# Windowed attention into an ELU feed-forward: one input load behind another gate, two value copies a step later, one subtraction behind two copies

## The chip, the cores and the metric

The kernel runs on one core of one Trainium2 chip. The metric is the device time of one execution in microseconds (us); three runs of the kernel before are given with their median. A profiled execution has its own time and, within it, a span from the first instruction to the last.

## The reference

The inputs are q, k and v of shape 8 x 8 x 576 x 64 (batch, heads, positions, width) in float32, and two matrices w_in (512 x 2048) and w_out (2048 x 512). Cut to what matters:

```
scores = q @ k.T / sqrt(64);  only |i - j| <= 32 is kept
attn = exp(scores) / sum(exp(scores));  y = attn @ v
x = y of all heads side by side: 4608 tokens x 512
h = x @ w_in
g = h where h > 0, else exp(min(h, 0)) - 1
out = g @ w_out            # 4608 x 512, float32
```

## The kernel before, in words

**Attention.** A batch has nine blocks of 64 query rows. Two blocks make a pair `i`, so 36 pairs cover the 8 batches, and four and a half pairs are one batch. `scores(i)` multiplies a 128-key window with the 64 queries of each block on TensorE (PE), for eight heads. `exponential(i)` is one exp on ScalarE (ACT), `mask(i)` multiplies with the band mask on VectorE (DVE), `pv(i)` multiplies with the values on PE, and `normalize(i)` divides by the sums on DVE. The result `x_st` is transposed, by PE for the first pairs (`x_transpose`, and a copy `x_evac` out of PSUM), later by DMA.

Even and odd blocks need the values at row offsets that differ by 64. So the values exist twice in SBUF: `V_e`, loaded by GpSimd's DMA queue with a conversion to bf16 (`load_v`, five parts for a batch), and `V_o`, the same rows moved by 64 partitions. `rotate_v(b, m0, m1, parts)` makes `V_o` with DVE copies (line 176); its part z of the copy reads parts m0 + z to m1 + z of `V_e`. `hold_v` is a tiny DVE write into `V_e` that a following `load_v` has to wait for, which sets the time at which GpSimd issues that load.

Queries and keys come in float32 through SyncE's DMA queue (`load_qk`, two transfers for each call, one for even and one for odd heads), are cast to bf16 (`cast_qk`) and transposed (`transpose_qk`) on PE for the early batches. Batch 1 comes in two parts: `ONE_A` through GpSimd's queue with a conversion, and `ONE_B`, the second part, in float32 through SyncE's queue.

**Feed-forward.** Tokens go in 18 tiles of 256. A tile has 8 steps, each of which takes 256 of the 2048 hidden columns. There are 144 steps `kk`; `order` lists which tile and which columns a step has. The first 16 steps mix tiles 0 and 1, ending with (tile 0, columns 7) at step 14 and (tile 1, columns 7) at step 15. In a step `mm1` (products, line 755) makes h in a PSUM bank; ACT makes exp(h) (`exponents`, line 764); DVE (ACT in three early steps) subtracts one (`subtract`, line 775) and `elu` (line 786) takes min and max into bf16 `g_sb`. Two steps later `mm2` adds g @ w_out into the tile's sums `psY` (line 806); after a tile's last `mm2`, `rows_out` copies both halves of the sums out of PSUM, one on ACT and one on DVE, and SyncE's queue writes them to memory. The h banks are `h0` and `h1`, by the parity of the step. Pair scores use bank pairs `s` and `u`; the bank pair `u` is lent to tile 1's sums (`h2` and `t0`) from step 5 to step 18 (`swap_pools`, `swap_back`).

**Order of the work.** Nothing is scheduled automatically: each engine runs its instructions in the order in which the program issues them. The loop over `kk` runs, in this order: the tasks "first", `elu` of the step before, the tasks "dve", `mm1` of this step with the tasks "half" in its middle, the tasks "mid", `mm2` of the step two before, and the tasks "end". `at(kk, slot, fn, ...)` puts a task into such a slot. So step 14's "mid" holds the cast of batch 1's second queries (on ACT), step 15's "mid" that of its keys (on DVE), and the ends of steps 15 and 16 hold their transposes; pairs 6 and 7 are scored in the middle of step 18.

**Gates.** The loads of the weights (`load_w_in`, `load_w_out`, in halves of quarters) and of batch 1's values are issued by GpSimd in a fixed order. `gate(src)` is a DMA of one element on SyncE's queue that reads `src`; as SyncE's queue waits for the landing of what the gate reads, everything behind it on this queue is issued only after that. In the kernel before one gate on the last column of w_in's fourth quarter (`w_in_at(3)`) stands ahead of the loads of batch 1's second part and of batch 2:

```python
    gate(w_in_at(3))
    for which in range(2):
        load_qk(1, which, ONE_B)
    for which in range(2):
        load_qk(2, which, WHOLE)
```

Of the kernel before, what the change touches and what calls it, by code (L numbers as in the profile page):

```python
# [15 lines left out]
def _bap(ap, new_ap, off=0):  # L16
    return bass.AP(tensor=ap.tensor, offset=ap.offset + off,
                   ap=[list(x) for x in new_ap])
# [3 lines left out]
def kernel(  # L22
# [15 lines left out]
    D_MODEL = H * D  # L38
# [8 lines left out]
    VS = 5  # L47
# [5 lines left out]
    NFO = D_FF // 128  # L53
# [56 lines left out]
    w_out_sb = wpool.tile([128, NFO, D_MODEL], BF16, name="w_out_sb")  # L110
# [10 lines left out]
    ONE_A, ONE_B = (0, HJ - 1), (NC * (HJ - 1), HJ + 1)  # L121
    qk_f = {}

    def load_qk(b, which, part, engs=(nc.sync, nc.sync)):
        z, nj = part
        mj = max(nj, HJ + 1)
        t = lpool.tile([128, 2, mj * D], FP32, tag=f"f{which}{mj}",
                       name=f"f{which}", bufs=2 if part is WHOLE else 1)
        qk_f[b, which, z] = t
        src = (q, k)[which][b, :, z:z + NC * nj, :].rearrange(  # L130
            "(g h) (c j) d -> c g h (j d)", h=2, j=nj)
        for h in range(2):
            engs[h].dma_start(out=t[:, h, 0:nj * D], in_=src[:, :, h, :])
# [14 lines left out]
    def load_v(b, m, rows=(0, 128)):  # L148
        lo = 128 * m - WIN
        p0 = max(rows[0], -lo)  # L150
        p1 = min(rows[1], S - lo)
        nc.gpsimd.dma_start(  # L152
            out=V_e[b % 3][p0:p1, m, :, 0:D],
            in_=v[b, :, lo + p0:lo + p1, :].rearrange("h p d -> p h d"))
# [37 lines left out]
    def gate(src, dt=BF16, eng=nc.sync):  # L192
        gates[0] += 1
        t = cpool.tile([1, 1], dt, name=f"gate{gates[0]}")
        eng.dma_start(out=t, in_=src)
# [17 lines left out]
    def w_in_at(c):  # L213
        return w_in_sb[0:1, 0, (c + 1) * (D_FF // 4) - 1:(c + 1) * (D_FF // 4)]
# [7 lines left out]
    def edges(i, eng=nc.vector):  # L222
        eng.memset(V_e[i][:, :, :, D:VD], 1.0)
        eng.memset(V_e[i][0:32, 0], 0.0)
        eng.memset(V_e[i][96:128, VS - 1], 0.0)
        if i < 2:
            for c0, n in ((KPAD - WIN, HP), (KPAD + HP * S, 1)):
                z = kT[i][:, c0:c0 + WIN]
                nc.vector.memset(_bap(z, [z.ap[0], [S, n], [1, WIN]]), 0.0)
# [328 lines left out]
        load_v(1, 2 + z)  # L558
    load_v(1, 4)
    edges(2, nc.gpsimd)  # L560
    gate(w_in_at(3))
    for which in range(2):
        load_qk(1, which, ONE_B)
    for which in range(2):
        load_qk(2, which, WHOLE)

# [5 lines left out]
    def at(kk, slot, fn, *args):  # L572
        tasks.setdefault((kk, slot), []).append((fn, args))
# [24 lines left out]
    def transpose_casts():  # L598
        elu(8)
        n, (nq, nk) = ONE_A[1], (c[1] for c in FRONT_C)  # L600
        pt = ps_tile([128, 2048], BF16, "s", "ptx")
        evicts = []
        for b, which, part, lo in ((0, 0, FRONT_C[0], n),
                                   (0, 1, FRONT_C[1], n + nq),
                                   (1, 0, ONE_A, 0)):
            transpose_qk(b, which, part, 0, part[1], nc.vector, later=evicts,
                         pt=pt[:, lo * 128:(lo + part[1]) * 128])
        pk = ps_tile([128, 1024], BF16, "h0", "ptx")
        transpose_qk(1, 1, ONE_A, 0, n, nc.scalar, later=evicts, pt=pk)
        for evict in evicts:  # L610
            evict()
# [11 lines left out]
        at(16 + m, "mid", load_v, 2, m)  # L623
    at(12, "dve", rotate_v, 1, 0, 1)
    for z in range(2):
        at(14 + z, "dve", rotate_v, 1, 1, VS - 1, (z,))

# [4 lines left out]
    for i in range(4, NPAIR):  # L634
        two = i >= FIRST_TWO
        kk, z = begin[i], i % 2 if two else 0
# [69 lines left out]
    def mm1(kk):  # L706
        t, s = order[kk]
        if kk == BY_PAIRS[1]:
            return
        ks = BY_PAIRS if kk == BY_PAIRS[0] else (kk,)  # L710
        tags = ((f"h{kk % 2}", "s") if kk == NSTEP - 1 else
                ("s",) if kk == 2 else ("u",) if kk == 3 else (f"h{kk % 2}",))
        for k in ks:
            psH[k] = []
        rows = 128 if kk >= BY_ROWS else TT
        for z, tag in enumerate(tags):
            for k in ks:
                psH[k].append(ps_tile([128, FG * TT // rows // len(tags),
                                       rows], FP32,
                                      tag if k == kk else "u", "ps"))  # L720
        for p in range(len(ks)):
            for k in ks:
                for z in range(len(tags)):
                    products(k, z, p if len(ks) > 1 else None)
                if p == len(ks) - 1:
                    for z in range(len(tags)):
                        exponents(k, z)
                        if k == NSTEP - 1:
                            elu(k, z)
# [31 lines left out]
    def exponents(kk, z):  # L761
        ps = psH[kk][z]
        e_sb = mpool.tile(list(ps.shape), FP32, tag="e_sb", name="e_sb")
        nc.scalar.activation(e_sb, ps, AX.Exp)  # L764
        e_t[kk, z] = e_sb
        if kk > 0:
            subtract(kk, z)

    def subtract(kk, z):
        e_sb = e_t.pop((kk, z))  # L770
        m_sb = mpool.tile(list(e_sb.shape), BF16, tag="m_sb", name="m_sb")
        if kk in (1, 3, 4):
            nc.scalar.activation(m_sb, e_sb, AX.Copy, bias=-1.0)
        else:
            nc.vector.tensor_scalar(m_sb, e_sb, -1.0, None, ALU.add)  # L775
        m_t[kk, z] = m_sb

    def elu(kk, z=0):
        ps = psH[kk][z]
        w, rows = ps.shape[1:]  # L780
        if z == 0:
            g_t[kk] = mpool.tile([128, FG * TT // rows, rows], BF16,
                                 tag="g_sb", name="g_sb", bufs=8)
        if kk == 0:
            subtract(kk, z)
        nc.vector.scalar_tensor_tensor(  # L786
            g_t[kk][:, z * w:(z + 1) * w, :], ps, 0.0, m_t.pop((kk, z)),
            ALU.max, ALU.min)
# [69 lines left out]
    for kk in range(NSTEP):  # L858
        run(kk, "first")
        for n in {1: (), 2: (0, 1), 9: ()}.get(kk, (kk - 1,)):  # L860
            if n >= 0:
                elu(n)
        run(kk, "dve")
        mm1(kk)
        run(kk, "mid")
        if kk == NSTEP - 1:
            last_sums()
        elif kk >= LATE + LAG:
            for _ in range(3 if kk < LATE + LAG + 4 else 4):
                add(*todo.pop(0))  # L870
        else:
            for n in {2: (), 3: (), 4: (), 5: (0, 2), 6: (1, 3), 7: (4,),
                      8: (5, 6)}.get(kk, (kk - LAG,) if kk >= LAG else ()):
                run(kk, n)
                mm2(n)
        run(kk, "end")
# [30 lines left out]
```

## Time and profile before

| | |
|---|---|
| median of three runs | 301.27 us (301.15 to 303.06) |
| the profiled execution's own time | 304.11 us |
| its span | 302.4 us |
| PE busy | 290.8 us, 96% |
| DVE busy | 240.7 us, 80% |
| ACT busy | 169.0 us, 56% |
| GpSimd busy | 56.5 us, 19% |
| granted clock of TensorE | full |

A busy share is an average over stages with different limits. The chain that ended last (PE 81%, DMA 11% of it) and the waits of single instructions tell what a stage is bound by. In the profile L755 and L806 are the products and the sums, L764 the exponent, L775 the subtraction, L786 the minimum and maximum, L291 and L293 copies and casts on ACT and on DVE, L341 and L385 PE's transposes and scores, L133 the float32 loads, L152 the value loads, L195 a gate. q0 is the queue of the DMAs that GpSimd issues, q1 that of SyncE and ACT. PEld is the loading of weights into TensorE, which overlaps the matmuls.

### The profile page before, as it was taken

Reading aid. Unit: us, or ns where it says so; the run is one execution under the profiler, and the core shown is the slowest. Engines: PE = TensorE matmul, PEld = TensorE weight load, DVE = VectorE, ACT = ScalarE, POOL = GpSimd, SP = SyncE. Lnnn points to the kernel's source line nnn. Section 1 sums busy time; section 2 is a strip of 40 time slices with the busy share of each in tenths; the row PEclk is TensorE's granted clock in tenths of the full one; section 3 lists DMA queues with packets and bytes.
Section 4 is the critical chain, followed back from the end, with each engine's and each line's share of the span. In section 5 each row is a group of like instructions: output and inputs, shape, how many; then the busy total and the mean of one; then the engine's idle time right before and its main releaser. Section 6 shows DMA issues by size and latency. Waiting matters only on the chain.

```text
span 302.4 us, 7697 instructions
## 1 busy us (share of the span) xinstructions
PE 290.8 (96%) x3080; PEld 198.2 (66%) x3132; DVE 240.7 (80%) x478; ACT 169.0 (56%) x256; POOL 56.5 (19%) x81
## 2 busy tenths in 40 slices
PE   7799998999999999999999999999999999999996
PEld 3476666677666666666666666666666666666764
DVE  7676787878888887988798879887888777777773
ACT  3774447778664567546753675377635363634342
POOL 8778611820004100230013001400000000000000
PEclk9999999999999999999999999999999999999999
DMA  9999999999965997999799969996941121121011
GB/s 192 170 190 164 186 222 410 374 165 201 200 196 148 297 121 198 261 310 149 134 259 287 237 154 274 315 171 118 259 81 72 35 72 36 72 37 69 2 69 70
DMA packets 94790, 52.74 MB, mean 174 GB/s; under 512 B 78243, under 2 KB 84643, under 8 KB 94755
## 3 DMA queue, kind: packets, MB, share of 16 engines
q0 software_dynamic: 45552, 10.03, 44.8%
q1 hardware_dynamic: 47330, 35.68, 44.7%
q10 hardware_dynamic: 1872, 6.55, 6.2%
q8 instruction: 24, 0.39, 0.5%
q14 instruction: 12, 0.09, 0.1%
HBM read 36.70 MB, written 15.34 MB: 172 GB/s over the span
## 4 chain that ended last, share of the span: by engine, by line
PE 81%; DMA 11%; POOL 3%; issue 2%; DVE 1%; ACT 1%; SPq 0%; POOLq 0%; DVEq 0%; ACTq 0%
PE ps L755 38%; PE psY L806 36%; DMA w_in_sb<-in_moe_w_in_dram 6%; PE psS L417 3%; PE psS L385 3%; DMA c<-in_q_dram 2%; DMA f<-in_q_dram 2%; POOL Vo L159 1%; PE ptx L341 1%; PE psXT L439 0%; POOL c L146 0%; DVE y_sb L293 0%; ACT e_sb L764 0%; DVE g_sb L786 0%; DVE m_sb L775 0%
## 5 line engine op out<-in xcount | busy, mean ns | idle before, releaser
L755 PE MATMUL ps<-xT,w_in_sb 128*128 128x256 bf16 (+1 forms) x1184 | 149.7, 270 | 0.5 <-DMA w_in_sb<-in_moe_w_in_dram 0.5
L764 ACT ACTIVATE e_sb<-ps 128x512 f32<-128x512 f32 (+1 forms) x145 | 86.1, 595 | 112.9 <-PE ps L755 106.0
L806 PE MATMUL psY<-w_out_sb,g_sb 128*128 128x512 bf16 (+2 forms) x541 | 139.0, 373 | 2.8 <-issue 0.3
L755 PEld LDWEIGHTS <-w_in_sb 128*128 128x128 bf16 x1184 | 110.9, 98 | 37.3 <-DMA w_in_sb<-in_moe_w_in_dram 0.6
L786 DVE SCALAR_TENSOR_TENSOR g_sb<-ps,m_sb 128x512 bf16<-128x512 f32 (+1 forms) x145 | 99.3, 686 | 13.2 <-DVE m_sb L775 0.5
L775 DVE TENSOR_SCALAR m_sb<-e_sb 128x512 bf16<-128x512 f32 (+1 forms) x142 | 61.2, 431 | 34.1 <-ACT e_sb L764 31.8
L806 PEld LDWEIGHTS <-g_sb 128*128 128x128 bf16 x592 | 55.8, 98 | 38.4
L152 POOL DMA_DIRECT2D Ve<-in_v_dram x37 | 32.1, 878 | 128.8 <-PE psS L417 79.5
L396 ACT ACTIVATE pu<-psS 128x1024 bf16<-128x1024 f32 x36 | 36.5, 1020 | 1.4 <-PE psS L385 1.4
L291 ACT CAST qkb<-f 128x768 bf16<-128x768 f32 (+2 forms) x29 | 25.1, 864 | 1.5 <-DMA f<-in_q_dram 1.5
L429 DVE TENSOR_TENSOR x_st<-psS,rc 128x512 bf16<-128x512 f32 x36 | 24.9, 691 | 1.2
L405 DVE TENSOR_TENSOR pm<-pu,masks 128x1024 bf16<-128x1024 bf16 x32 | 21.8, 681 | 0.5 <-ACT pu L396 0.5
L417 PEld LDWEIGHTS <-pm 128*64 128x64 bf16 x512 | 9.6, 111 | 7.3 <-DVE pm L405 6.9
L293 DVE COPY y_sb<-psY 128x512 f32<-128x512 f32 (+1 forms) x18 | 12.2, 676 | 1.4 <-PE psY L806 1.4
L385 PEld LDWEIGHTS <-kT 64*128 64x128 bf16 x560 | 9.4, 95 | 4.8 <-issue 4.0
L291 ACT COPY y_sb<-psY 128x512 f32<-128x512 f32 (+1 forms) x19 | 10.8, 567 | 2.8 <-PE psY L806 2.8
L385 PE MATMUL psS<-qT,kT 64*128 64x64 bf16 x560 | 11.9, 191 | 0.4
L417 PE MATMUL psS<-Ve,pm 128*64 128x65 bf16 x288 | 11.5, 196 | 0.1
L417 PE MATMUL psS<-Vo,pm 128*64 128x65 bf16 x224 | 10.3, 196 | 0.0
L176 DVE COPY Vo<-Ve 64x1040 bf16<-64x1040 bf16 (+2 forms) x22 | 9.1, 413 | 0.7
L291 ACT COPY qT<-ptx 128x512 bf16<-128x512 bf16 (+4 forms) x7 | 6.3, 936 | 4.1 <-PE ptx L341 2.7
L426 DVE RECIPROCAL rc<-psS 128x8 f32<-128x8 f32 x36 | 7.1, 198 | 1.5 <-PE psS L417 1.4
(58 smaller groups left out, 94.0 us busy)
## 6 DMA issues: line engine op xcount, KB each, us to landing
out_dram<-y_sb SPq DMA_DIRECT2D x35, 256.0 KB, 3.8
f<-in_q_dram SPq DMA_DIRECT2D x12, 576.0 KB, 6.7
f<-in_k_dram SPq DMA_DIRECT2D x12, 576.0 KB, 8.3
in_dram<-qkb ACTq DMA_DIRECT2D x10, 576.0 KB, 4.2
Ve<-in_v_dram POOLq DMA_DIRECT2D x21, 128.0 KB, 12.1
w_out_sb<-in_moe_w_out_dram POOLq DMA_DIRECT2D x8, 256.0 KB, 8.7
Ve<-in_v_dram POOLq DMA_DIRECT2D x14, 96.0 KB, 10.8
w_in_sb<-in_moe_w_in_dram POOLq DMA_DIRECT2D x5, 256.0 KB, 8.0
```

The lines of the kernel that those rows point to most:

```text
L152: nc.gpsimd.dma_start(out=V_e[b % 3][p0:p1, m, :, 0:D], in_=v[b, :, lo + p0:lo + p1, :].rearrange("h p d -> p h d"))
L291: nc.scalar.copy(d_, s_)
L385: nc.tensor.matmul(psS[:, h % 2, hp * 128 + z * QB:hp * 128 + (z + 1) * QB], lhsT=keys, rhs=qT[b % 2][base:base + 64, hp, QB * qb:QB * (qb ...
L396: nc.scalar.activation(pu, _bap(psS, [psS.ap[0], [1, 1024]]), AX.Exp, scale=SCALE)
L405: nc.vector.tensor_mul(pm, pu, _bap(mm, [mm.ap[0], [0, H], [1, 2 * QB]]))
L417: nc.tensor.matmul(psS[QB * z:QB * (z + 1), par, hp * VD:(hp + 1) * VD], lhsT=pm[:, par * HP + hp, z * QB:(z + 1) * QB], rhs=vv[:, qb // 2 ...
L429: nc.vector.tensor_mul(x_st, _bap(psS, [psS.ap[0], [VD, HP], [512, 2], [1, D]]), _bap(rc, [rc.ap[0], [2, HP], [1, 2], [0, D]]))
L755: nc.tensor.matmul(o, lhsT=w_in_sb[:, do, fo * 128:(fo + 1) * 128], rhs=r, start=(do == 0), stop=(do == NDO - 1))
L764: nc.scalar.activation(e_sb, ps, AX.Exp)
L775: nc.vector.tensor_scalar(m_sb, e_sb, -1.0, None, ALU.add)
L786: nc.vector.scalar_tensor_tensor(g_t[kk][:, z * w:(z + 1) * w, :], ps, 0.0, m_t.pop((kk, z)), ALU.max, ALU.min)
L806: nc.tensor.matmul(sum_of(t, ts, c), lhsT=(g_t[n][:, j, :] if n >= BY_ROWS else g_t[n][:, j, ts * 128:(ts + 1) * 128]), rhs=w_out_sb[:, fi ...
```

## The change

Three edits:

- SyncE's queue has two gates. The first reads the last element of w_out's third quarter and stands ahead of the queries of batch 1's second part; the second is the gate on w_in's fourth quarter, now ahead of the keys of that part and of batch 2.
- The two DVE copies that make the rest of batch 1's `V_o` (`rotate_v(1, 1, 4, (z,))`) go from steps 14 and 15 to steps 15 and 16.
- Step 17's subtraction is issued ahead of its `elu` in step 18, as step 0's already is, and not right behind its exponent. Between the two places `mm2` of step 15 issues tile 1's copies out of PSUM, so on DVE the copy comes first and the subtraction after it.

```diff
@@ loads
     edges(2, nc.gpsimd)
+    gate(w_out_sb[0:1, 3 * NFO // 4 - 1, D_MODEL - 1:D_MODEL])
+    load_qk(1, 0, ONE_B)
     gate(w_in_at(3))
-    for which in range(2):
-        load_qk(1, which, ONE_B)
+    load_qk(1, 1, ONE_B)
     for which in range(2):
         load_qk(2, which, WHOLE)
@@ tasks
     for z in range(2):
-        at(14 + z, "dve", rotate_v, 1, 1, VS - 1, (z,))
+        at(15 + z, "dve", rotate_v, 1, 1, VS - 1, (z,))
@@ exponents
         e_t[kk, z] = e_sb
-        if kk > 0:
+        if kk not in (0, 17):
             subtract(kk, z)
@@ elu
-        if kk == 0:
+        if kk in (0, 17):
             subtract(kk, z)
```

## The prediction

> **What bounds the kernel now.** I read the page first (PE busy 96% of 302.4 us, the chain that ended last 81% PE), then the chain of waits around the edited lines, then the timelines of PE, ACT, DVE, POOL and SP over 20 to 60 us, and last the DMA answers of short windows. TensorE is the bound almost everywhere: a step costs about 1.74 us in the middle of the run (starts of its first products at 91.26, 93.00, 94.74). So only a hole on PE can be won. The largest one after the start is beside the change, and the chain names its cause:
>
> ```profile
> 30.16 9.05 DMA w_in_sb<-in_moe_w_in_dram
> 39.21 0.02 issue
> 39.23 0.75 SPq L195
> ...
> 40.12 0.57 SPq L133
> 40.69 0.04 issue
> 40.74 6.68 DMA f<-in_q_dram
> ...
> 47.56 1.10 issue
> 48.66 0.59 ACT xT L291
> 49.25 0.04 issue
> 49.29 0.73 PE ptx L341 x10
> ```
>
> Columns: start, length, what. The last w_in copy lands at 39.21, SP's gate lets the query load go, its second half lands at 47.42, ACT casts it, ACT copies xT, and only then PE transposes the queries. The timelines of ACT and PE show the price (number in brackets: idle before):
>
> ```profile
> 47.49 1.26 ACT L291 CAST qkb<-f 128x1280 bf16<-128x1280 f32 x1 [1.55 <-DMA f<-in_q_dram]
> 48.66 0.58 ACT L291 COPY xT<-psXT 128x512 bf16<-128x512 bf16 x1
> ...
> 47.78 0.38 PE L806 MATMUL psY<-w_out_sb,g_sb 128*128 128x512 bf16 x1
> 49.29 0.72 PE L341 MATMUL ptx<-ident,qkb 128*128 128x128 bf16 x10 [1.13 <-ACT xT L291]
> ```
>
> PE has 1.13 us of nothing; matmuls overlap, and in an unbroken flow the next starts 0.22 after the last (47.78), so 48.00 against 49.29: 1.29 us to be had. The cast matters twice: it makes the transposes' input, and the xT copy stands behind it on ACT, whose bank "s" the transposes reuse. A smaller hole is step 18, in the weight loads:
>
> ```profile
> 54.84 0.29 PEld L385 LDWEIGHTS <-kT 64*128 64x128 bf16 x16 [0.21 <-issue]
> 55.39 0.29 PEld L385 LDWEIGHTS <-kT 64*128 64x128 bf16 x16 [0.26 <-DVE y_sb L293]
> ```
>
> Pair 7's scores need the bank pair "u", and tile 1's sums leave it only when DVE has copied them. DVE, in order:
>
> ```profile
> 54.10 0.65 DVE L775 TENSOR_SCALAR m_sb<-e_sb 128x512 bf16<-128x512 f32 x1 [0.67 <-ACT e_sb L764]
> 54.67 0.67 DVE L293 COPY y_sb<-psY 128x512 f32<-128x512 f32 x1
> ```
>
> The subtraction of step 17 waits for ACT, and the copy, whose sums were ready at about 53.9 (mm2 of step 15 starts at 53.0 and takes 0.87), stands behind it.
>
> **What the skill says.** The Trainium skill, DMA: Bandwidth & Descriptors, section "Queues, rings and completion order": each DMA engine takes turns between the queues that have work, a packet of descriptors at a time. The trace agrees: in 42.0 to 43.5 both queues move:
>
> ```profile
> q0 software_dynamic: 1014, 0.13, 134.0%
> q1 hardware_dynamic: 96, 0.23, 50.3%
> ```
>
> The same section says that a semaphore is full only when all engines have landed; here the four ONE_B issues land 5.4, 6.7, 6.8 and 7.0 us after they are issued although a pair's 640 KB needs some 2 us at the 330 GB/s that the windows show for 44 to 46, so the slowest engine decides. PSUM — Partial Sum Buffer, "Engine vs sequencer instructions": ScalarE and VectorE queues are strict FIFO; the xT and y_sb waits above are just that.
>
> **The change part by part.**
>
> *Queries earlier.* The gate now reads w_out's third quarter, whose last copy is issued at 28.02 and lands 9.0 later: 37.02. SP's gate takes 0.75 and starts 0.14 before the loads follow, so the query halves go out at 37.9 and 38.5, not 40.12 and 40.74: 2.2 us sooner. From issue to the first packet was 1.9 us (40.12 to 42.0), so packets begin at 39.8. There they meet the value and w_out copies of POOL, which fill q0 until about 43.75. Under that contention q1 moved 17 packets per quarter us in 42.5 to 43.25; the queries are 256 packets (two halves, 128 partitions): 256 / 17 x 0.25 = 3.8 us, with the slow start of that window some 4.3, so 44.1. In the run before the 256th packet came at about 45.1 and the landing was at 47.42, 2.3 later; 44.1 + 2.3 = 46.4 is my landing. Bounds: 45.0 (as quickly after issue as before, 38.5 + 6.7 = 45.2) and 47.4 (the engines are busy in both cases, nothing is won). Step 14's exponent ends at 45.95 on ACT. Cast and xT take 1.17 + 0.63, so PE at 48.0 is not held if the cast starts by 46.2. At 46.4 some 0.2 of the 1.29 remain: gain 1.1. Ends: 1.29 and 0.
>
> *Keys.* SP's second gate waits for the same w_in landing (39.21), so the key halves go out at 40.1 and 40.7, 1.35 sooner (two query issues no longer stand before them). They landed at 48.25 and 49.05. The engines have the same bytes to move ahead of them, so I take no gain from bandwidth and little from order: 48.3 to 49.1. DVE casts them behind step 15's subtraction; that was 50.11 and will be about 48.55, as ACT and PE have moved up. A wait of up to 0.5 on DVE follows. Behind it stand step 15's g_sb, hold_v, the values' copy, step 16's m_sb, tile 0's y_sb and g_sb; PE's step 18 products want that g_sb (their bank) at 52.7, and I get it at 52.3 with no wait and 52.8 with 0.5. Cost 0.1; ends 0 and 0.5.
>
> *POOL's copies made later.* Nothing of POOL's is moved in its queue, but q0 runs at 57% beside q1 (150 packets a quarter us against 261). From 39.8 it had 2.2 us of its own and 1.0 us worth spread over the contention, 3.2 in all; 3.2 / 0.57 = 5.6, so 45.4 and not 43.75. The last w_in landed at 39.21 and is untouched. w_out's last eighth (34.48 + 8.3 = 42.8) becomes 44.3 and is wanted at 49.5. Values part 3 (35.94 + 8.1 = 44.0) becomes 45.6, part 4 (44.9) 46.5. No cost.
>
> *Copies of the values a step later.* Two DVE copies of 0.56 go from steps 14 and 15 to 15 and 16. At 45.01 the first would have waited 0.6 for part 3; at 47.2 and 50.0 both are free of waits. In step 15 DVE would idle for e_sb anyway (1.64 idle at 49.77 before), in step 16 the copy lies in 50.05 to 50.6, ahead of e_sb at 50.6. First reader is pair 6's product of step 20. hold_v stays ahead of it, so POOL's next loads go out with the shift. Cost 0, or 0.5 if the cover is gone.
>
> *Subtraction behind tile 1's copies.* No instruction more or fewer. y_sb can start at 52.85 (mm2 of step 15 ends 1.2 sooner), ends 53.5; pair 7's scores want it at 54.0. m_sb and g_sb then end at 54.6; PE wants that bank at 55.3 and the sum a step later. The 0.26 hole goes: gain 0.2; ends 0 and 0.26.
>
> Sum: 1.1 + 0.2 - 0.1 = 1.2 us. The extra gate on SP (0.75) lies in its idle time before 39. From 56 us on PE is dense (39.42 of 40 us in 60 to 100), the casts, stores and transposes hang on steps and move with them, batch 2's queries and keys land 5 us or more before their casts (51.1 at the latest against 56.32 for the queries), and its values are issued on hold_v, which moves along. So it reaches the end. Profiled execution: 304.11 with span 302.4, to 302.9 and 301.2. The median before is 301.27, 2.84 below that execution; the same 1.2 off gives 300.1.
>
> **Rivals.**
> 1. *Hidden anyway* (300.8 to 301.9, middle 301.3). The engines are full from 20 to 50 us, so an earlier issue need not be an earlier landing: queries at 47.4, or keys at 50.3, take the gain back. For it: bytes conserved. Against it: queries now are alone in q1 for 2.2 us.
> 2. *Slower.* Keys (or values) land so late that DVE's queue holds PE. Beyond 48.9 each us costs PE one; it passes the gain of 1.3 at 50.2 and costs 1% at 53.3. Cause would be q0 and q1 sharing the engines longer, with the slowest engine last. Middle case, landing at 52: +1.8, 303.1. Against it: they go out 1.35 sooner and landed by 49.05.
> 3. *Only the small part works* (301.05): queries as late as before, y_sb hole gone. It lies within rival 1's range.
>
> **Numbers.** Forecast 0.68 (own range 299.5 to 300.8); rivals 1 and 3 together 0.22; slower 0.10, of which 0.06 beyond 1%. Range 299.5 to 302.0: the forecast's, with the rival of no gain and a little of the slow one. Less than 1% (3.0 us) is about what a measurement of this kernel can tell from no change, and no hole here is that large: faster 0.01, within 0.93, slower 0.06.
>
> **What would show it.** Right: query issue at about 37.9 on SP, cast on ACT at 45.95 to 46.5 with little idle, PE's query transposes at 48.0 to 48.3 with no idle over 0.3, no wait of L385 for y_sb, span near 301.2. Wrong: the cast still idle over 1 us for f; DVE's key cast waiting over 1 us for f<-in_k_dram; a DVE copy of Vo waiting for Ve; w_out or w_in among PE's waits after 40 us.

## The result, and the profile after

The changed kernel is slower by 4%: a median of 314.04 us (313.48 to 315.14, six runs) against 301.27 (300.90 to 303.06, six runs), ratio 1.0416 with a 95% interval of 1.0384 to 1.0448. Its profiled execution took 313.98 us with a span of 312.3; it is typical, while the profiled execution of before (304.11) was not, which matters below.

The queries are there in time, as forecast. From the timelines of ACT and PE of the changed kernel (start, length, engine, line; in brackets the idle time before, and what ended it):

```profile
44.56 1.25 ACT L291 CAST qkb<-f 128x1280 bf16<-128x1280 f32 x1
45.83 1.03 PE L807 MATMUL psY<-w_out_sb,g_sb 128*128 128x512 bf16 x4
46.69 0.72 PE L341 MATMUL ptx<-ident,qkb 128*128 128x128 bf16 x10
```

The cast has no idle time before it, and PE goes from the sums to the transposes without a hole. The loss comes from a part that the prediction put at no cost: the landing of batch 1's values. The chain of waits of the changed kernel over 20 to 60 us:

```profile
by line: DMA Ve<-in_v_dram 81.3%; PE ps L756 5.2%; issue 4.3%; POOL Ve L152 2.3%; POOL c L146 1.7%; POOL w_out_sb L208 1.7%; DVE y_sb L293 1.5%; DVE Vo L176 1.5%; DVE m_sb L776 1.1%; POOL w_in_sb L200 0.4%
...
34.73 23.98 DMA Ve<-in_v_dram
58.70 0.02 issue
58.73 0.58 DVE Vo L176
```

Part 4 of batch 1's values takes 24 us from issue to landing, where it took 8.1 before; part 3 takes 16.4 and lands at 50.2. DVE stands with both copies at the head of its queue, and behind each of them the step's subtraction and g_sb:

```profile
50.29 0.56 DVE L176 COPY Vo<-Ve 64x1560 bf16<-64x1560 bf16 x1 [4.37 <-DMA Ve<-in_v_dram]
...
58.73 0.58 DVE L176 COPY Vo<-Ve 64x1560 bf16<-64x1560 bf16 x1 [5.95 <-DMA Ve<-in_v_dram]
```

On PE this makes two holes, before the keys' transposes and before step 18's products, which need the bank that step 16's g_sb frees:

```profile
52.10 0.73 PE L341 MATMUL ptx<-ident,qkb 128*128 128x128 bf16 x10 [2.95 <-DVE qkb L293]
...
61.02 1.89 PE L756 MATMUL ps<-xT,w_in_sb 128*128 128x256 bf16 x8 [5.08 <-DVE g_sb L787]
```

The second line shows one thing more: eight products take 1.89 us, not 1.04. PE's table by stretches (length, busy us and count, granted clock, DMA share, GB/s) says why:

```profile
54.00:55.00 1.00, 1.00 (x5) 0.50 1.05 412
...
62.00:63.00 1.00, 1.00 (x13) 0.50 5.07 72
63.00:64.00 1.00, 1.00 (x33) 0.50 4.79 99
```

After each hole the clock is granted at half. PE works at half clock for about 8.6 us (53.1 to 55.9 and 61.0 to 66.7). If that work took twice its time, 4.3 us are lost, and with 2.95 + 5.08 of holes this estimate comes to 12.3. From step 15's first product to step 20's PE takes 23.1 us here and 10.9 in a typical execution of before (g1 below): 12.2. The holes and the slow clock are nearly the whole loss, which is 12.5 us between these two spans; from step 20 to 30 both kernels take the same (22.2 and 22.3).

Why the values were late is in the queues' lines (packets, MB, packet time as a share of 16 engines). The changed kernel at 47 to 48 us:

```profile
q1 hardware_dynamic: 95, 0.40, 101.5%
q0 software_dynamic: 34, 0.00, 6.5%
```

And before, at 57 to 58, at 60 to 61 and at 64 to 65 us, where batch 2's values are under way:

```profile
q1 hardware_dynamic: 94, 0.36, 96.4%
q0 software_dynamic: 91, 0.01, 17.6%
...
q1 hardware_dynamic: 161, 0.30, 92.7%
q0 software_dynamic: 164, 0.02, 31.8%
...
q0 software_dynamic: 1217, 0.15, 254.0%
```

The pairs to see are 94 and 91, 161 and 164: beside SyncE's queue, GpSimd's moves one packet for each of the other's, whether those are mostly loads of 4608 bytes or stores of 2048, and a value packet is 128 bytes. Alone it moves 1217 in the same time. So even a full q0 falls to 7.5 and 13.5% of its rate beside q1 in these two stretches, and these lines were in the profile before the change.

In the changed kernel the pair is 95 and 34, not one for one, and q0's count falls to 12 by 54 us. A reading that fits is that most of the 16 engines are through with their share of the values and only the rest still take turns; the trace does not name the engine of a packet, so this is inferred from counts. It is plainest in h1 below, at 49 to 50 us, and in e3 below at 46 to 47, where q1 is empty:

```profile
q1 hardware_dynamic: 100, 0.42, 105.2%
q0 software_dynamic: 5, 0.00, 1.0%
...
q0 software_dynamic: 57, 0.01, 11.1%
```

A sixteenth of 100 is 6, and a sixteenth of 1217 is 76 (e3's 57 were through by 46.7). By this estimate about one engine's leftover decides when a part has landed. GpSimd was not behind in issuing, as its last issue ends at 35.51; and DVE's work did not hold the packets up: DVE stood idle from 45.9 to 50.3, and q0 moved only 31 to 34 a us from 45 to 50.

### The profile page after: what moved, and what is told of

It reads as the page before. It is cut to its first block, busy times and chain, and to the rows that moved or that the text cites. A ratio compares the mean times of both kernels' runs of the same rounds, so it can differ in the third digit from the quotient of the medians.

```text
span 312.3 us, 7751 instructions
## 1 busy us (share of the span) xinstructions
PE 298.2 (96%) x3132; PEld 199.5 (64%) x3132; DVE 240.6 (77%) x478; ACT 169.2 (54%) x256; POOL 56.2 (18%) x81
## 4 chain that ended last, share of the span: by engine, by line
PE 83%; DMA 12%; POOL 2%; DVE 1%; issue 1%; ACT 0%; POOLq 0%
PE ps L756 38%; PE psY L807 36%; DMA Ve<-in_v_dram 10%; PE psS L417 3%; PE psS L385 3%; DMA c<-in_k_dram 2%; PE psXT L439 1%; PE ptx L341 1%; POOL Vo L159 1%; POOL Ve L152 0%; POOL c L146 0%; PE psS L365 0%; POOL w_out_sb L208 0%; PE ptx L336 0%; DVE g_sb L787 0%
## 5 line engine op out<-in xcount | busy, mean ns | idle before, releaser
L756 PE MATMUL ps<-xT,w_in_sb 128*128 128x256 bf16 (+1 forms) x1184 | 151.6, 272 | 5.1 <-DVE g_sb L787 5.1
L807 PE MATMUL psY<-w_out_sb,g_sb 128*128 128x512 bf16 (+2 forms) x592 | 149.0, 377 | 0.0
L176 DVE COPY Vo<-Ve 64x1040 bf16<-64x1040 bf16 (+2 forms) x22 | 9.1, 414 | 10.9 <-DMA Ve<-in_v_dram 10.3
L293 DVE COPY y_sb<-psY 128x512 f32<-128x512 f32 (+1 forms) x18 | 12.2, 677 | 1.4 <-PE psY L807 1.4
L385 PE MATMUL psS<-qT,kT 64*128 64x64 bf16 x560 | 12.1, 194 | 0.1
L417 PE MATMUL psS<-Vo,pm 128*64 128x65 bf16 x224 | 10.3, 196 | 0.0
L291 ACT COPY kT<-ptx 128x1152 bf16<-128x1152 bf16 (+4 forms) x6 | 6.1, 1024 | 5.7 <-PE ptx L341 3.2
L341 PE MATMUL ptx<-ident,qkb 128*128 128x128 bf16 x74 | 5.6, 220 | 3.6 <-DVE qkb L293 3.5
```

The costliest lines, as they stand in the source:

```text
L291: nc.scalar.copy(d_, s_)
L385: nc.tensor.matmul(psS[:, h % 2, hp * 128 + z * QB:hp * 128 + (z + 1) * QB], lhsT=keys, rhs=qT[b % 2][base:base + 64, hp, QB * qb:QB * (qb ...
L417: nc.tensor.matmul(psS[QB * z:QB * (z + 1), par, hp * VD:(hp + 1) * VD], lhsT=pm[:, par * HP + hp, z * QB:(z + 1) * QB], rhs=vv[:, qb // 2 ...
L756: nc.tensor.matmul(o, lhsT=w_in_sb[:, do, fo * 128:(fo + 1) * 128], rhs=r, start=(do == 0), stop=(do == NDO - 1))
L807: nc.tensor.matmul(sum_of(t, ts, c), lhsT=(g_t[n][:, j, :] if n >= BY_ROWS else g_t[n][:, j, ts * 128:(ts + 1) * 128]), rhs=w_out_sb[:, fi ...
```

## The experiments

Each edit is shown against the changed kernel, cut to its changed lines. Ratios are to the kernel before, measured beside each experiment (its medians there are 301.59 to 301.87). The table gives the start of the first product of some steps on PE, from the traces:

| kernel | step 15 | 16 | 18 | 19 | 20 | 30 |
|---|---|---|---|---|---|---|
| before, the profile shown | 46.01 | 49.84 | 53.88 | 56.61 | 58.34 | 80.58 |
| before again (g1) | 44.80 | 47.34 | 51.37 | 53.97 | 55.70 | 78.01 |
| changed | 44.73 | 47.25 | 61.02 | 65.49 | 67.83 | 90.06 |
| e1 gate alone | 44.38 | 55.91 | 62.23 | 64.66 | 66.40 | 88.63 |
| e2 gate late | 44.28 | 46.84 | 50.87 | 53.28 | 55.02 | 77.25 |
| g3 copies where due | 44.34 | 46.86 | 50.89 | 53.31 | 56.25 | 79.56 |

**e1, the earlier gate alone.**

```diff
@@ tasks
-        at(15 + z, "dve", rotate_v, 1, 1, VS - 1, (z,))
+        at(14 + z, "dve", rotate_v, 1, 1, VS - 1, (z,))
@@ exponents
-        if kk not in (0, 17):
+        if kk > 0:
@@ elu
-        if kk in (0, 17):
+        if kk == 0:
```

> Only the earlier gate for the queries; the value copies are back in steps 14 and 15 and step 17's subtraction is back behind its exponent. Theory (the float32 loads of q1 came in before GpSimd's value copies were through, and those then got only a packet in turn until the float32 loads ran out): the values' parts 3 and 4 land as late as in the changed kernel, near 50 and 59 us, DVE waits for them one step sooner, so PE loses a step (1.7 us) more: 314 to 317. Rival (the copies put a step later, or the subtraction, made the stall): 300 to 301.5.

Measured: 312.46 us, ratio 1.0358 (1.0332 to 1.0383). The earlier gate by itself makes the loss; e2 shows that the other two edits don't. The size was missed: it is a little less than in the changed kernel, not more. Its copies wait longer (7.42 and 4.74 us, 12.2 together against 10.3), but PE does less work at half clock: it starts again at 52.2 and has the full clock from about 55.5 on. Putting the copies a step later did not shield anything.

**e2, the gate late.** Both gates read w_in's fourth quarter; the rest of the change stays.

```diff
-    gate(w_out_sb[0:1, 3 * NFO // 4 - 1, D_MODEL - 1:D_MODEL])
+    gate(w_in_at(3))
```

> The changed kernel, but the first gate reads w_in's fourth quarter as well, so the queries go out after the same landing as before; two gates, late copies and late subtraction stay. Theory: the values are through before the float32 loads start, no wait of Vo copies for Ve, the hole of 1.1 us before the queries' transposes is back, tile 1's y_sb wait is gone: 300.8 to 301.6. Rival (the second gate or the later copies and subtraction carry the loss): 305 or more.

Measured: 302.09 us, ratio 1.0010 (0.9997 to 1.0024), half a us above the expected range. The second gate, the later copies and the later subtraction are free. But the hole before the queries' transposes did not come back, though the queries went out at 38.13 and not at 35.92: step 15 to 16 takes 2.56 us, and the cast waits 0.27.

**e3, batch 2 held back** until part 4 of batch 1's values has landed.

```diff
     load_qk(1, 1, ONE_B)
+    gate(V_e[1][0:1, 4, 0, 0:1])
     for which in range(2):
         load_qk(2, which, WHOLE)
```

> The changed kernel with a third gate, on part 4 of batch 1's values, ahead of batch 2's float32 loads. Theory (the values starve for as long as q1 has packets): q1 then holds only the 512 packets of queries and keys, some 4 us; the values crawl for that time and finish in 2 us after it, parts 3 and 4 near 46 and 47; no long wait of the Vo copies, 299.5 to 301.5. Rival (the values are late because the queries went ahead of them, whatever follows; or their own queue is held): still over 306.

Measured: 302.02 us, ratio 1.0019 (1.0001 to 1.0038); a shade above the expected range, and the loss is gone. The timeline of DVE:

```profile
46.61 0.56 DVE L176 COPY Vo<-Ve 64x1560 bf16<-64x1560 bf16 x1 [1.02 <-DMA Ve<-in_v_dram]
...
49.01 0.55 DVE L176 COPY Vo<-Ve 64x1560 bf16<-64x1560 bf16 x1
```

The queries went out at 35.96, as in the changed kernel. Parts 3 and 4 now take 13.0 and 12.7 us and not 16.4 and 24.0: the values wait for as long as q1 has something to move, not because the queries went ahead.

**e4, the values ahead of w_out's last eighth** in GpSimd's order.

```diff
-    for z in range(2):
-        load_w_out(3, z, 2)
-        load_v(1, 2 + z)
-    load_v(1, 4)
+    load_w_out(3, 0, 2)
+    for m in (2, 3, 4):
+        load_v(1, m)
+    load_w_out(3, 1, 2)
```

> The changed kernel with the last eighth of w_out issued by GpSimd behind the values' parts 3 and 4 and not between parts 2 and 3. Theory (turns are taken by packets, so what is left in q0 counts by its number of packets: 256 of 1024 bytes for that eighth against 1792 of 128 bytes for the two value parts): the values are through at about 42, w_out's eighth takes 4 to 6 us beside q1 and lands by 48, wanted at 49: 299.5 to 301.5. Rival (bytes decide, the last copy in q0 waits until q1 is empty): w_out lands near 58 and PE waits for it in step 16: 308 or more.

Measured: 301.88 us, ratio 1.0000 (0.9986 to 1.0014). No copy waits, and w_out's eighth, now last in q0 beside q1, took 10.3 us against 8.9 in the changed kernel. The queues' lines of 42 to 43 us:

```profile
q1 hardware_dynamic: 153, 0.34, 89.9%
q0 software_dynamic: 32, 0.03, 17.0%
```

q0 moves as few packets as the changed kernel's q0 did at 47 to 48, but they are of 1024 bytes, and the copy has 256 of them where two value parts have 1792. What is caught in the slow stretch counts by its packets, not by its bytes. The time is 0.4 us above the expected range; there is no hole to be won, see g1. And with the values out of the way the early issue won nothing: the queries went out at 35.84 and landed at 44.88, in g1 at 37.97 and 44.38.

**g1, the kernel before, once more.** No edit.

> The kernel before, unchanged, profiled once more. Theory (the 1.1 us hole ahead of the queries' transposes was a matter of that one execution, which ran 2.8 us above the median): step 15 to step 16 on PE takes 2.3 to 3.0 us and the cast waits under 0.6 us for the queries, span near 299.5. Rival (the hole is there in every execution and the gain was lost elsewhere): step 15 to 16 takes 3.8 us as in the first profile.

Measured: 301.52 us in one run, span 299.8. PE's timeline:

```profile
45.92 1.03 PE L806 MATMUL psY<-w_out_sb,g_sb 128*128 128x512 bf16 x4
46.78 0.72 PE L341 MATMUL ptx<-ident,qkb 128*128 128x128 bf16 x10
```

No hole: step 15 to 16 takes 2.54 us, against 3.83 in the profile that the prediction was built on. The difference is the 1.29 us that the queries' part was to win; of all executions traced, only that one had this hole (at most 0.33 us of it is left in another, e4).

**g2, a gate between the two:** the first gate on part 1 of the values.

```diff
-    gate(w_out_sb[0:1, 3 * NFO // 4 - 1, D_MODEL - 1:D_MODEL])
+    gate(V_e[1][0:1, 1, 0, 0:1])
```

> The changed kernel with the first gate on part 1 of batch 1's values, which lands between w_out's third quarter and w_in's fourth. Theory (whatever value packets are left when q1 starts on an engine wait until q1 runs empty, so the loss is a cliff): part 3 is through, part 4 lands at 55 to 59 as in the changed kernel, one long wait of 6 to 9 us: 307 to 312. Rival (loss in proportion to how much earlier the loads start): about 305, part 4 near 50.

Measured: 301.55 us, ratio 0.9997 (0.9981 to 1.0014). The queries go out at 37.48, 1.56 later than in the changed kernel, and no copy waits. The expected 307 to 312 was missed: part 4 took 10.5 us, not over 20. Of the gates tried, this one is on the safe side and none gave a loss halfway, so whether there is a cliff is not shown.

**g3, the copies where their readers need them.**

```diff
-    for z in range(2):
-        at(15 + z, "dve", rotate_v, 1, 1, VS - 1, (z,))
+    at(18, "dve", rotate_v, 1, 1, VS - 1, (0,))
+    at(19, "dve", rotate_v, 1, 1, VS - 2, (1,))
+    at(24, "dve", rotate_v, 1, VS - 2, VS - 1, (1,))
```

> The changed kernel with the value copies where their first reader needs them: parts 1 to 3 into the lower half in step 18, parts 2 and 3 into the upper half in step 19, part 4's copy alone in step 24 (its reader is pair 8, step 28). Theory (values late by 10 to 20 us cost only because DVE's queue stands behind them): landings stay near 50 and 59 us, no wait over 0.5 us, 300.5 to 302.5. Rival (the float32 loads and the values slow each other down for all, or w_out's last part is late as well): over 305.

Measured: 303.48 us, ratio 1.0058 (1.0036 to 1.0081). The values land as late as in the changed kernel (16.9 and 24.1 us after issue), no copy waits for them, and 10 of the 12 us are back. So most of the loss is not the lateness itself but DVE's queue standing behind the copies. The range was missed by a us, since the copies now lie in a full stretch of DVE, and PE shows it in step 20:

```profile
56.25 1.03 PE L757 MATMUL ps<-xT,w_in_sb 128*128 128x256 bf16 x8 [1.04 <-DVE g_sb L788]
```

**g4, smaller packets:** batch 2's and 3's float32 loads cut in two by rows.

```diff
-            engs[h].dma_start(out=t[:, h, 0:nj * D], in_=src[:, :, h, :])
+            if part is WHOLE and b in (2, 3):
+                for j in (0, HJ):
+                    engs[h].dma_start(out=t[:, h, j * D:(j + HJ) * D],
+                                      in_=src[:, :, h, j * D:(j + HJ) * D])
+            else:
+                engs[h].dma_start(out=t[:, h, 0:nj * D], in_=src[:, :, h, :])
```

> The changed kernel with the float32 loads of batches 2 and 3 cut in two by rows, so that their packets are 2304 and not 4608 bytes. Theory (the queues take turns by packets): beside these loads q0 moves about twice the 34 packets a us that it moved at 47 to 48 us, 60 to 75; part 3 lands a little sooner, part 4 still when q1 runs empty, so the time stays at 311 to 315. Rival (turns by bytes, or q1 ahead of q0 by rank): q0 stays at 30 to 40 packets a us.

Measured: 305.53 us in one run, against an expected 311 to 315; the copies wait 3.00 and 0.36 us. Part 4 landed at 52.7, while q1 was still full, and not when q1 ran empty. At 47 to 48 us:

```profile
q1 hardware_dynamic: 185, 0.38, 103.2%
q0 software_dynamic: 30, 0.00, 5.7%
```

q1's packets doubled and q0's did not, which is against my reading of turns; that part 4 took 16.4 us and not 24.0 is for it. How many of the 16 engines still held value packets may differ from run to run, and only those can take turns. The pairs in the profile of before, where q0 was full, stay the better evidence. This one is inconclusive.

**h1, a gate on an earlier copy:** w_in's fourth quarter, first half.

```diff
-    gate(w_out_sb[0:1, 3 * NFO // 4 - 1, D_MODEL - 1:D_MODEL])
+    gate(w_in_sb[0:1, 0, 7 * D_FF // 8 - 1:7 * D_FF // 8])
```

> The changed kernel with the first gate one weight copy earlier still, on the first half of w_in's fourth quarter (issued just ahead of w_out's third quarter's last copy), so the queries go out some 2 us sooner. Theory (what is left in q0 when q1 takes its turn is what starves): more values, and w_out's last copies too, are caught: part 3 and 4 wait as long or longer, 313 to 320. Rival (the queries' first packets move at 40 us whenever they are issued, so it makes no difference to the changed kernel): 312.5 to 314.5, same landings.

Measured: 313.69 us, ratio 1.0388 (1.0362 to 1.0414), the copies wait 6.63 and 4.79. It was to be 2 us earlier and was not: the gate behind that copy starts at 35.26, no sooner than the gate behind the one issued after it in the changed kernel (35.04). The expected ranges of theory and rival both hold 313.69, so it repeats the changed kernel and doesn't extend the series.

Over all runs, what separates the two outcomes is the time between the end of GpSimd's last value issue and the queries' issue: -0.2 to 0.9 us in the six whose last two parts take 12.7 us and more (changed, e1, e3, g3, g4, h1), and 1.7 to 2.8 us in those where they take 10.5 us and less (g2, g1, before, e2). In e4, whose last issue is not a value part, it doesn't apply. This was found afterwards; no run tests it as a cause.

## Why the prediction was wrong

**The step that failed** is "POOL's copies made later", with its "no cost". It took q0's rate beside q1 as 57%, from 150 packets a quarter us against 261 (the window's three quarters have 167, 155 and 145, which is 60%). That window (42.5 to 43.25) was the start of the overlap, when q1 moved only 17 packets a quarter us; so it, and the 1014 beside 96 that the prediction shows, have both queues moving but say nothing of their turns. In the full overlap of 57 to 58 us of the same trace q1 moved 94 a us and q0 91 against 1217 alone. With 57% part 3 came out at 45.6 and part 4 at 46.5; they landed at 50.2 and 58.7. From this follows the second cost of nothing, for the two copies a step later, that were to be "free of waits" and waited 4.37 and 5.95 us. That is one of the signs of being wrong that the prediction names. Rival 2 had the right place (DVE's queue held by a load) in its brackets: values rather than keys. Its price, 1.8 us at a landing of 52, was far off for what came, because q1 holds more than the queries and keys: all of batch 2's and 3's loads follow without a gap, and e3 shows that this following traffic decides.

The prediction also draws on the Trainium skill for what a landing is: only the full count of the semaphore says that all data has landed. The page (DMA: Bandwidth & Descriptors) states this in "Why a DMA increments its semaphore by 16 and not by 1", not in the section that the prediction names. The counts of h1 and e3 agree with it, by the estimate above: about one engine's share was still on its way. The prediction used one rate for all of q0.

**Cover lost.** I asked whether the two copies would wait and not what would be behind them if they did. The part on the copies gave 0.5 us for the lost cover; it was 10.3 us of DVE and, through the clock, 12.2 on PE. The Trainium skill, TensorE: Matmul & The Clock Gate, "Part 1: The HAM clock gate", says that the clock falls to half after an idle window of about 3.4 us and comes back after as long a busy one. The trace agrees on the half (0.50), and a hole of 2.95 us, with transposes behind it, was enough here. No step of mine priced a hole above its own length.

**Queries earlier.** The landing was to be 1.0 us sooner (46.4 against 47.42); it came at 43.39 against 44.38 in g1, also 1.0, and the cast no longer waits. But the gain of 1.1 did not exist. The sum was made against one execution 2.84 us above the median, and the hole was part of what made it slow; g1 and e2 are without it. The prediction named the difference and subtracted it at the end as if it lay elsewhere.

**Subtraction behind the copies.** Forecast 0.2. Step 18 to 19 takes 2.60 us in g1 and 2.41 in e2, 0.19 less (2.42 in e3, e4, g2 and g3). Right, and too small for the medians: e2's interval includes no change.

**Keys.** They were cast at 51.22, behind the late copy, so 0.1 for their own landing can't be read from this run. The extra gate on SyncE's queue cost nothing, as said (e2).

**The rest.** PE's density after 56 us was read rightly: the 12.1 us by which step 20 starts later than in g1 are 12.1 at step 30 and 12.5 at the end of the span. The rival "hidden anyway" is what the versions without late values give: e4 and g2 are at the time of before. No version tried beats it. What stays open is why 1.6 us in the queries' issue flips the outcome and why an engine or a few are left behind: in the changed kernel and in g2 alike q1's first query packets move at 40 us, and which engines then still hold value packets isn't in the trace.

## What to carry to other kernels

Before moving a load ahead of others, count the packets that will still be in the other queue, and take their rate from a stretch in which both queues are full; here copies in small packets lost almost all of theirs beside large ones (34 of 1217 a us) and got it back when the large ones ended. Keep a copy that depends on a late transfer out of the head of an engine's queue until its reader is near, or hold the following bulk loads behind it. And before a hole is booked as a gain, see it in a second execution, above all when the profiled one is slower than the median.

## What the runs showed of the hardware

Two queues that share the DMA engines went packet for packet (94 and 91, 161 and 164 in a us), so 128-byte packets fell from 1217 a us to 91; late in a transfer, 5 a us beside 100, about a sixteenth, were enough to hold up a landing (h1). From a float32 load's issue to its first packet there were 1.9 us in one execution of before and 4.2 in the changed kernel, while q0 was full. And holes of 2.95 and 5.08 us on PE were followed by about 3 and 6 us of work at half clock.
